# A different order of VectorE's work at the ends of groups, and of the first two units' scores, in a fused attention and SwiGLU kernel

## The chip, the core and the metric

The kernel runs on one core of one Trainium2 chip. The metric is the device time of one execution in microseconds (us). The kernel before takes 995.05 us, the median of three runs (994.68 to 995.08). The profile is of one execution with a span of 992.9 us from the first to the last instruction; times inside it count from the start of that span.

## The reference: hashed attention, then a SwiGLU block

The inputs are q, k and v of 4 batches, 8 heads, 768 positions and 64 dimensions, a projection of 64 x 6, two weights of 512 x 1536 and one of 1536 x 512. Cut to what matters:

```python
q_bucket = sum(((q @ proj) > 0) * 2**arange(6))      # k_bucket likewise
scores = where(q_bucket[:, None] == k_bucket[None, :], q @ k.T / 8, -1e9)
attn = softmax(scores)                               # with 1e-9 added to the sum
x = (attn @ v) with heads side by side               # (3072, 512)
g = x @ w_gate
out = (g * sigmoid(g) * (x @ w_val)) @ w_out         # (3072, 512)
```

## The kernel before

Heads are handled in pairs, 16 pairs in all, four to a batch. A pair has two halves of 384 queries, a half has six units of 128 keys. For a unit, `score` puts q k^T of two heads into two PSUM banks, adds a product of hash bits that pushes down the pairs whose buckets differ, and lets ScalarE take the exponential. All these banks come from one pool of seven that are handed out in turn:

```python
banks = tile_pool(name="ps", bufs=7, space=PSUM)

def score(u):
    sc = [bank("sc")[:, 0:HQ] for _ in range(2)]
    for x, start in ((T, True), (bits, False)):
        if u < 2 and not start:
            prepare_pair(1)          # units 0 and 1: the transposes of the second halves of k, of q
        for h in range(2):
            nc.tensor.matmul(sc[h], x["k", n][rows, ks], x["q", n][rows, qs], start=start, stop=not start)
    for h in range(2):
        nc.scalar.activation(weights(u)[:, h, 0:HQ], sc[h], AF.Exp, ...)
```

`prepare_pair` issues the next step of a pair's preparation: a transpose of three blocks on TensorE and its copy on ScalarE into `qT` or `kT`, or a hash product (`hps`) and the signs of it on ScalarE. For the first pair the hash of the second halves is issued after unit 2.

The SwiGLU block of a batch follows when its four pairs are done, beside the attention of the next batch. It is cut into atoms in a list, and after each attention step some atoms are taken from the list. Both its products use Strassen's scheme with seven products in place of eight. The up product (`up`) has six groups of two hidden tiles each, f and f + 1, and two halves of the tokens, so four spots (m, half) for the gate (g = 0) and four for the value (g = 1). For batches after the first a group is nested: two of its seven products are split by the scheme once more (`deeper`, width 192), which needs sums of weight blocks (`weigh`, into `inner` or `words`). Those of the first nested product are the group's `ahead` work:

```python
ahead = [lambda: weigh(0)] if nested else []        # four sums of 128 x 128 on VectorE

def step(at):
    if at == 0:
        while first: first.pop(0)()                 # operand sums of the batch
        finish(ahead)
    for do in todo[at]: do(at)                      # products, adds of PSUM into tiles, copies
    if at == len(todo) - 1:
        look_ahead()                                # the next atom's ahead work, if it has any
        settle(at + NB)                             # the group's last gating operations

def look_ahead():
    if atoms:
        finish(getattr(atoms[0][1], "ahead", []))
```

A gating is ScalarE's tanh, then two operations on VectorE: `c<-th,c` (line 571) and `hid<-c,hid` (line 575). The adds of PSUM into tiles, the weight sums and the operand sums are all `plus` (line 597 in the profile), and the matmuls of both products are `product` (line 593).

The down product (`po`) of a batch has three chunks of tokens with seven products each. Its operand sums are made by `combine` in two parts, part 0 by `early()` at the last up atom and part 1 in the first down step:

```python
def chunk(i):
    def step(n):
        a11, a12, s3, a22 = parts(i, slice(None))
        if n == 0 and i == 0:
            while next(preparing, None): pass
            for which in (1, 2, 3): combine(0, which, 1)
        ...
        a, w, to = ((a11, b11, "a"), (s1, t1, "b"), (s2, t2, "a"), (a12, b21, "c"),
                    (s3, t3, "a"), (s4, b22, "b"), (a22, t4, "a"))[n]
        product(now[to], [(a[:, f], w[:, f]) for f in range(NFP)], n in (0, 1, 3))
        ...                                         # copy or add to the output tile, send it
        for part in range(2):
            if n == 0: combine(i, 4, part)
            elif n in (3, 4) and i + 1 < CH:
                for which in ((1,), (2, 3))[n - 3]: combine(i + 1, which, part)
    for n in range(NB):
        atoms.append((2, lambda n=n: step(n), n == NB - 1))

def push_ffn(b):
    up_strassen(x, b, first)
    at = len(atoms) - 1
    early = down_strassen(out_of)
    size, last, end = atoms[at]
    atoms[at] = (size, lambda: (early(), last()), end)
```

When the attention is over, the rest of the list, above all the six up groups and the down product of the last batch, is run by the last lines:

```python
for _, atom, _ in atoms:
    atom()
```

[...]

Of the kernel before, what the change touches and what calls it, by code (L numbers as in the profile page):

```python
# [13 lines left out]
AF = mybir.ActivationFunctionType  # L14
# [4 lines left out]
def kernel(  # L19
# [11 lines left out]
    nc = tc.nc  # L31
    PSUM = bass.MemoryType.PSUM
    B, H, S, D = q.shape
# [3 lines left out]
    CH = NCH // 2  # L37
    HQ = CH * P
    BLOCK = 32
    NP = H // 2  # L40
# [10 lines left out]
    OFF = 2.0**35  # L51
    SCALE = 1.0 / D**0.5
# [16 lines left out]
    def bank(name):  # L69
        return banks.tile([P, 512], FP32, tag="ps", name=name)  # L70
# [98 lines left out]
    for h in range(2):  # L169
        rows = slice(h * D, (h + 1) * D)  # L170
# [24 lines left out]
    NB = 7  # L195
# [67 lines left out]
    def as_words(t):  # L263
        return t.bitcast(I32).rearrange("p (f w) -> p f w", w=2)

    spots = [hid[:, half, m].rearrange("p f q -> p (f q)") for half in range(2) for m in range(2)]
    early = [as_words(t[:, 0 : 2 * PIECE]) for t in spots]
# [115 lines left out]
    T = {}  # L383
    bits = {}
    atoms = []
# [85 lines left out]
    units = [(n, half, c) for n in range(len(pairs)) for half in range(2) for c in range(NCH)]  # L471
# [9 lines left out]
    def weights(u):  # L481
        return ((early_ring if u < MOVE else late_ring) + ring)[u % NCH]

    def score(u):
        n, half, c = units[u]
        qs = slice(half * HQ, (half + 1) * HQ)
        ks = slice(c * P, (c + 1) * P)
        sc = [bank("sc")[:, 0:HQ] for _ in range(2)]
        for x, start in ((T, True), (bits, False)):
            if u < 2 and not start:  # L490
                prepare_pair(1)
            for h in range(2):
                rows = slice(h * D, (h + 1) * D)
                nc.tensor.matmul(sc[h], x["k", n][rows, ks], x["q", n][rows, qs],  # L494
                                 start=start, stop=not start)
        for h in range(2):
            nc.scalar.activation(weights(u)[:, h, 0:HQ], sc[h], AF.Exp,  # L497
                                 scale=SCALE * (OFF / 2 if n <= NP else 1.0))

    def attend(u):  # L500
        n, half, c = units[u]
# [27 lines left out]
    def total(n):  # L529

        b, pr = pairs[n]

        ps = av_ps.tile([P, 512], FP32, tag="av", name="sum") if b == 0 else bank("sum")
        t = [acc.pop((n, half)) for half in range(2)]
        for h in range(2):
            for half in range(2):
                g = (2 * h + half) * BLOCK
                nc.tensor.matmul(ps[g : g + BLOCK, 0:HQ], ones, t[half][:, h, :],  # L540
                                 start=True, stop=True)
        if b == 0:
            space = wo.rearrange("p f m -> p (f m)")
            space = space[:, n % 2 * 3 * HQ : (n % 2 + 1) * 3 * HQ].rearrange("p (x q) -> p x q", q=HQ)
            r, t = space[:, 2, :], space[:, 0:2, :]
        else:
            r, t = t[1][:, 0, :], t[0]
        nc.vector.reciprocal(r, ps[:, 0:HQ])
        for half in range(2):
            for h in range(2):  # L550
                g = (2 * h + half) * BLOCK
                for at in (h * D, h * D + BLOCK):
                    nc.sync.dma_start(t[at : at + BLOCK, half, :], r[g : g + BLOCK, :])
        waiting.append(lambda: norm(n, t))
        if pr == NP - 1:
            push_ffn(b)
# [33 lines left out]
    def product(ps, pairs_, start):  # L590

        for i, (a, x) in enumerate(pairs_):
            nc.tensor.matmul(ps, a, x, start=start and i == 0, stop=i == len(pairs_) - 1,  # L593
                             skip_group_check=True)

    def plus(o, a, b, op=ALU.add):
        nc.vector.tensor_tensor(o, a, b, op=op)  # L597
# [162 lines left out]
        for i in range(NG // 2):  # L760
            both(i)

    def down_strassen(out_of):


        t2, t3, t4 = down_t
        t1 = b12
        s2, s1, s4 = down_s

        def parts(i, fs):  # L770
            return [hid[:, half, m, fs, i * P : (i + 1) * P]
                    for half in range(2) for m in range(2)]

        def combine(i, which, part):
            fs = slice(part * NFP // 2, (part + 1) * NFP // 2)
            a11, a12, a21, a22 = parts(i, fs)
            if which == 1:
                plus(s1[:, fs], a21, a22)
            elif which == 2:
                plus(s2[:, fs], s1[:, fs], a11, ALU.subtract)  # L780
            elif which == 3:
                plus(a21, a11, a21, ALU.subtract)
            else:
                plus(s4[:, fs], a12, s2[:, fs], ALU.subtract)

        def chunk(i):
            now = {}

            def step(n):
                a11, a12, s3, a22 = parts(i, slice(None))  # L790
                if n == 0 and i == 0:
                    while next(preparing, None):
                        pass
                    for which in (1, 2, 3):
                        combine(0, which, 1)
                if n == 0:
                    for name in "cba":
                        now[name] = bank("po")[:, 0:HD]
                    o = word_room[0]
                    now["o"] = [[o[:, (2 * r + x) * HD : (2 * r + x + 1) * HD] for x in range(2)]  # L800
                                for r in range(2)]
                a, w, to = ((a11, b11, "a"), (s1, t1, "b"), (s2, t2, "a"), (a12, b21, "c"),
                            (s3, t3, "a"), (s4, b22, "b"), (a22, t4, "a"))[n]
                c = now[to]
                product(c, [(a[:, f], w[:, f]) for f in range(NFP)], n in (0, 1, 3))
                r, x = ((0, 0), (1, 1), (0, 1), (0, 0), (1, 1), (0, 1), (1, 0))[n]
                o = now["o"][r][x]
                if n in (3, 4, 5):
                    plus(o, o, c)
                else:  # L810
                    nc.scalar.copy(o, c)  # L811
                if n >= 3:
                    nc.sync.dma_start(out_of(r, i)[:, x * HD : (x + 1) * HD], o)
                for part in range(2):
                    if n == 0:
                        combine(i, 4, part)
                    elif n in (3, 4) and i + 1 < CH:
                        for which in ((1,), (2, 3))[n - 3]:
                            combine(i + 1, which, part)

            for n in range(NB):
                atoms.append((2, lambda n=n: step(n), n == NB - 1))

        for i in range(CH):
            chunk(i)
        return lambda: [combine(0, which, 0) for which in (1, 2, 3)]

    def push_ffn(b):
        x = [xT[b, pr] for pr in range(NP)]
        rows = out[b * S : (b + 1) * S, :].rearrange("(p c) m -> p c m", c=NCH)  # L830

        def out_of(half, i):
            return rows[:, half * CH + i, :]

        up_strassen(x, b, first)
        at = len(atoms) - 1
        early = down_strassen(out_of)
        size, last, end = atoms[at]
        atoms[at] = (size, lambda: (early(), last()), end)

# [6 lines left out]
    def prepare_pair(count):  # L849
        for _ in range(count):  # L850
            rest.extend(f for f in steps.pop(0)() or [] if f)
# [5 lines left out]
    for u in range(0, N, NCH):  # L857
        n, half, _ = units[u]
# [5 lines left out]
        for c in range(NCH):  # L864
            score(u + c)
            if u + c == 2 or not gating and half == 1 and c == 2:
                prepare_pair(1)
            if c == 1 and half == 0 and 0 < n <= NP:
                total(n - 1)
            if c:  # L870
                add(u + c)
# [36 lines left out]
        end = True  # L908
        part = 0
        while atoms and (credit > 0 or not end):  # L910
            size, atom, end = atoms.pop(0)
# [11 lines left out]
            for _ in range(size):  # L923
                if chores:
                    step = chores.pop(0)
                    chores.extend(step and step() or [])
        while chores:
            step = chores.pop(0)
            chores.extend(step and step() or [])
    for _, atom, _ in atoms:  # L930
        atom()


# [30 lines left out]
```

The softmax here doesn't subtract the row's maximum and nothing guards it: scores larger than these inputs give would overflow.

## Time and profile before

The page of the profile and the lists behind it give this:

| what | value |
|---|---|
| time, median of 3 | 995.05 us |
| span of the profile | 992.9 us |
| ScalarE's waits for PSUM of the down product (line 811) | 180.1 us, 45 times |
| VectorE's waits for PSUM of the up product (line 597) | 76.5 and 41.6 us |
| TensorE's granted clock | 0.999 |
| up groups of batch 3 | from 822 to 933 us |
| down product of batch 3 | from 934 to 990 us |

Busy time says how long an engine had an instruction under way, and an average over the span hides single stages. A wait names the engine whose signal came last. Waits of an engine that isn't the bound cost nothing by themselves: ScalarE's 180.1 us above are such waits. The chain of work that ended last goes back from the last instruction to what released it, step by step; TensorE holds 91% of it, VectorE 5%, ScalarE 2%. In such a list a line has the start in us, the length in us, and the engine, the source line and what is written there; "x68" counts instructions that are merged in one line. An fp32 matmul stands as two records of equal length.

### The profile page before, as it was taken

The page shows a single profiled execution, that of the slowest core. Times are in us where ns is not written, and L with a number is a line of the kernel's source. Part 1 is how long each engine was busy: PE and PEld are TensorE (multiplying, and loading weights), DVE is VectorE, ACT ScalarE, POOL GpSimd, SP SyncE. Part 2 cuts the span into 40 slices and gives each one's busy share as a digit, 9 for nine tenths or more (in the row PEclk, how much of TensorE's full clock was granted, in tenths as well). Part 3 has the DMA queues.
Part 4 walks back from the last instruction along what each step waited for, and adds up shares of the span by engine and source line. Part 5 has one row for each costly group of instructions (what it writes and reads, how often), then busy time and mean ns, then how long its engine had stood idle before and what let it go on. Part 6 is the DMA issues. An engine that isn't in the chain of part 4 may idle for free.

```text
span 992.9 us, 13575 instructions
## 1 busy us (share of the span) xinstructions
PE 980.0 (99%) x4813; PEld 625.0 (63%) x4813; DVE 670.4 (68%) x1276; ACT 408.1 (41%) x921; POOL 127.3 (13%) x248
## 2 busy tenths in 40 slices
PE   9999999999999999999999999999999999999998
PEld 4444555555577766656566775666666786666687
DVE  5899888888965556777784457776776446667631
ACT  7999555566512234444442313443342202323200
POOL 3222232231100011111010001111100001121000
PEclk9999999999999999999999999999999999999999
DMA  8777685875303042433322114343121112233001
GB/s 235 218 249 229 157 259 178 228 269 157 106 26 76 16 121 79 104 92 84 99 81 57 52 31 108 98 107 100 57 87 33 35 34 85 75 117 105 1 30 35
DMA packets 119987, 107.02 MB, mean 108 GB/s; under 512 B 90032, under 2 KB 104848, under 8 KB 119920
## 3 DMA queue, kind: packets, MB, share of 16 engines
q0 software_dynamic: 18336, 73.29, 23.0%
q1 hardware_dynamic: 100784, 32.67, 14.2%
q8 instruction: 38, 0.62, 0.3%
q10 hardware_dynamic: 800, 0.20, 0.1%
q14 instruction: 29, 0.24, 0.1%
HBM read 81.79 MB, written 17.30 MB: 100 GB/s over the span
## 4 chain that ended last, share of the span: by engine, by line
PE 91%; DVE 5%; issue 2%; ACT 2%; POOL 0%; DMA 0%; DVEq 0%; ACTq 0%; POOLq 0%
PE up L593 41%; PE po L593 21%; PE sc L494 14%; PE av L509 11%; PE sum L540 1%; PE hps L412 1%; DVE c L571 1%; DVE hid L575 1%; PE tps L396 1%; DVE hid L597 1%; DVE room L368 0%; DVE inner L597 0%; PE idle L134 0%; DVE acc L527 0%; ACT th L570 0%
## 5 line engine op out<-in xcount | busy, mean ns | idle before, releaser
L593 PE MATMUL up<-xT,room 128*128 128x384 f32 (+1 forms) x732 | 243.0, 465 | 0.0
L593 PEld LDWEIGHTS up<-xT,room 128*128 128x128 f32 x732 | 134.8, 190 | 73.3 <-issue 9.8
L593 PE MATMUL up<-xc,room 128*128 128x384 f32 (+1 forms) x540 | 176.9, 455 | 0.0
L327 POOL DMA_DIRECT2D room<-ram x144 | 77.9, 543 | 677.8 <-PE up L593 662.4
L494 PE MATMUL sc<-qT,kT 64*128 64x384 f32 x768 | 161.0, 494 | 0.0
L597 DVE TENSOR_TENSOR c<-c,up 128x192 f32<-128x192 f32 (+1 forms) x198 | 78.9, 406 | 80.9 <-PE up L593 76.5
L527 DVE TENSOR_TENSOR acc<-acc,A 128x768 f32<-128x768 f32 x128 | 122.7, 958 | 15.7 <-ACT A L497 2.9
L593 PEld LDWEIGHTS up<-xc,room 128*128 128x128 f32 x540 | 99.2, 190 | 43.8 <-DVE c L597 1.1
L570 ACT ACTIVATE th<-c 128x384 f32<-128x384 f32 x90 | 46.9, 522 | 158.1 <-DVE c L571 89.7
L497 ACT ACTIVATE A<-sc 128x384 f32<-128x384 f32 x256 | 103.9, 528 | 0.6 <-PE sc L494 0.5
L494 PEld LDWEIGHTS sc<-qT,kT 64*128 64x128 f32 x768 | 67.9, 186 | 54.3 <-issue 40.5
L811 ACT COPY words<-po 128x256 f32<-128x256 f32 x48 | 17.9, 373 | 199.0 <-PE po L593 180.1
L597 DVE TENSOR_TENSOR hid<-hid,up 128x192 f32<-128x192 f32 (+1 forms) x162 | 67.5, 418 | 43.5 <-PE up L593 41.6
L509 PE MATMUL av<-A,vraw 128*64 128x384 f32 (+1 forms) x512 | 88.2, 486 | 0.0
L597 DVE TENSOR_TENSOR words<-words,po 128x256 f32<-128x256 f32 x36 | 15.2, 421 | 99.2 <-PE po L593 99.2
L679 ACT COPY c<-up 128x384 f32<-128x384 f32 x72 | 34.4, 478 | 88.8 <-PE up L593 88.7
L593 PE MATMUL po<-wo,room 128*128 128x256 f32 x288 | 66.6, 380 | 1.5 <-DVE room L597 1.5
L593 PE MATMUL po<-wo,hid 128*128 128x256 f32 x288 | 66.9, 382 | 0.0
L593 PE MATMUL po<-room,hid 128*128 128x256 f32 x288 | 66.1, 379 | 0.0
L509 PEld LDWEIGHTS av<-A,vraw 128*64 128x64 f32 x512 | 36.7, 137 | 46.1 <-issue 44.1
L494 PE MATMUL sc<-qb,kb 64*128 64x384 bf16 x384 | 65.1, 323 | 0.5 <-DVE kb L426 0.5
L593 PEld LDWEIGHTS po<-wo,hid 128*128 128x128 f32 x288 | 54.1, 190 | 12.1 <-issue 4.9
(137 smaller groups left out, 1165.3 us busy)
## 6 DMA issues: line engine op xcount, KB each, us to landing
room<-ram POOLq DMA_DIRECT2D x96, 384.0 KB, 3.7
vraw<-in_v_dram SPq DMA_DIRECT2D x16, 384.0 KB, 3.3
ram<-room POOLq DMA_DIRECT2D x12, 512.0 KB, 5.1
room<-ram POOLq DMA_DIRECT2D x48, 128.0 KB, 3.5
out_dram<-words SPq DMA_DIRECT2D x48, 128.0 KB, 1.7
room<-in_moe_w_out_dram POOLq DMA_DIRECT2D x10, 512.0 KB, 6.4
qraw<-in_q_dram SPq DMA_DIRECT2D x48, 96.0 KB, 3.2
hid<-in_moe_w_gate_dram POOLq DMA_DIRECT2D x9, 512.0 KB, 6.8
```

What stands on the lines that cost most here:

```text
L327: nc.gpsimd.dma_start(places[k % 2][:, PARTS[go], :], ram[k % NG][:, PARTS[go], :])
L396: nc.tensor.transpose(ps[:, i * P : (i + 1) * P], raws[name, n][:, half * CH + i, :, :].rearrange("p h d -> p (h d)"), ident)
L412: nc.tensor.matmul(tile_[i * BLOCK : (i + 1) * BLOCK, 0:HQ], hash_w, T[name, n][:, half * HQ : (half + 1) * HQ], start=True, stop=True)
L494: nc.tensor.matmul(sc[h], x["k", n][rows, ks], x["q", n][rows, qs], start=start, stop=not start)
L497: nc.scalar.activation(weights(u)[:, h, 0:HQ], sc[h], AF.Exp, scale=SCALE * (OFF / 2 if n <= NP else 1.0))
L509: nc.tensor.matmul(ps[h * D : (h + 1) * D, 0:width], raws["v", n][:, h, c, :], a[:, h, 0:width], start=c == 0, stop=c == NCH - 1)
L527: nc.vector.tensor_tensor(acc[n, half], acc[n, half], a[:, :, 0:HQ], op=ALU.add)
L570: nc.scalar.activation(th, g, AF.Tanh, scale=0.5)
L593: nc.tensor.matmul(ps, a, x, start=start and i == 0, stop=i == len(pairs_) - 1, skip_group_check=True)
L597: nc.vector.tensor_tensor(o, a, b, op=op)
L679: nc.scalar.copy(tile_of(g, spot), c)
L811: nc.scalar.copy(o, c)
```

## The change

It moves instructions and neither adds nor removes any. There are four parts.

- The tail takes each atom off the list before it runs it, so that `look_ahead` finds the next group there. Its purpose is that the weight sums of the next group are formed ahead of the last gating operations of the group before.
- In the last batch's down product the first chunk runs its products in the order 0, 3, 1, 2, 4, 5, 6. Its purpose is to give VectorE time for the operand sums that product 1 reads.
- `early()` is called after the last up atom of a batch in place of before it, except for the last batch. Its purpose is that the operations which free PSUM banks and feed the last tanh come first.
- For the first pair, the scores of unit 1 and the transposes of the second halves of both k and q are issued ahead of the bits of unit 0.

```diff
+    open_scores = {}
     def score(u):
+        n = units[u][0]
+        if u == 0:
+            for v in range(2):
+                score_part(v, T, True)
+                prepare_pair(1)
+        elif u > 1:
+            score_part(u, T, True)
+        score_part(u, bits, False)
+        for h in range(2):
+            nc.scalar.activation(weights(u)[:, h, 0:HQ], open_scores[u][h], AF.Exp, ...)
+
+    def score_part(u, x, start):
         n, half, c = units[u]
-        sc = [bank("sc")[:, 0:HQ] for _ in range(2)]
-        for x, start in ((T, True), (bits, False)):
-            if u < 2 and not start:
-                prepare_pair(1)
-            ...                      # matmuls and exponentials, now in the two functions
+        if start:
+            open_scores[u] = [bank("sc")[:, 0:HQ] for _ in range(2)]
+        sc = open_scores[u]
         ...
-    def down_strassen(out_of):
+    def down_strassen(out_of, at_once):
         ...
-            def step(n):
+            order = (0, 3, 1, 2, 4, 5, 6) if at_once and i == 0 else range(NB)
+            def step(at):
+                n = order[at]
         ...
-                    elif n in (3, 4) and i + 1 < CH:
-                        for which in ((1,), (2, 3))[n - 3]:
+                    elif at in (3, 4) and i + 1 < CH:
+                        for which in ((1,), (2, 3))[at - 3]:
         ...
-        early = down_strassen(out_of)
+        early = down_strassen(out_of, b == B - 1)
         size, last, end = atoms[at]
-        atoms[at] = (size, lambda: (early(), last()), end)
+        atoms[at] = (size, lambda: (early(), last()) if b == B - 1 else (last(), early()), end)
     ...
-    for _, atom, _ in atoms:
-        atom()
+    while atoms:
+        atoms.pop(0)[1]()
```

More of the change, by code (lines that the diff above doesn't have):

```diff
@@ L482, in weights @@
         return ((early_ring if u < MOVE else late_ring) + ring)[u % NCH]
+    open_scores = {}
     def score(u):
+        n = units[u][0]
[7 more added lines that the diff above has]
+        for h in range(2):
+            nc.scalar.activation(weights(u)[:, h, 0:HQ], open_scores[u][h], AF.Exp,
+                                 scale=SCALE * (OFF / 2 if n <= NP else 1.0))
+    def score_part(u, x, start):
         n, half, c = units[u]
@@ L487, in score @@
         ks = slice(c * P, (c + 1) * P)
-        sc = [bank("sc")[:, 0:HQ] for _ in range(2)]
-        for x, start in ((T, True), (bits, False)):
-            if u < 2 and not start:
-                prepare_pair(1)
[L492 to L495, printed above, removed]
+        if start:
+            open_scores[u] = [bank("sc")[:, 0:HQ] for _ in range(2)]
+        sc = open_scores[u]
         for h in range(2):
-            nc.scalar.activation(weights(u)[:, h, 0:HQ], sc[h], AF.Exp,
-                                 scale=SCALE * (OFF / 2 if n <= NP else 1.0))
+            rows = slice(h * D, (h + 1) * D)
+            nc.tensor.matmul(sc[h], x["k", n][rows, ks], x["q", n][rows, qs],
+                             start=start, stop=not start)
     def attend(u):
```

## The prediction

> **What bounds the kernel now.** I read the page's busy times first, then what TensorE waited for by its own wait list, then the chain of work that ended last, and last the timelines around each place where that chain leaves TensorE.
>
> The first line is the page's busy time; the next three are from the list of who waited for whom, cut to TensorE (waited for, total us, times, longest):
>
> ```profile
> PE 980.0 (99%) x4813; PEld 625.0 (63%) x4813; DVE 670.4 (68%) x1276; ACT 408.1 (41%) x921; POOL 127.3 (13%) x248
> ...
> PE up L593 <- DVE inner L597: 5.7, 5, 1.1
> PE po L593 <- DVE room L597: 1.5, 2, 1.0
> PE sc L494 <- DVE kb L426: 0.5, 1, 0.5
> ```
>
> TensorE is the bound over nearly all of the 992.9 us span, so no change that leaves its matmuls alone can win more than its holes. The list names them: five waits for VectorE's `inner` (the weight sums of the next group), two for `room` (the operand sums of the down product), one at the start for `kb` (the keys' bits).
>
> [...] a hole is larger than the wait shown. I therefore measure holes by starts. From the chain that ended last (start, us, what):
>
> ```profile
> 351.16 17.48 PE up L593 x68
> 368.64 5.05 PE sc L494 x36
> ...
> 507.17 3.47 PE sc L494 x21
> 510.64 0.04 issue
> 510.68 2.30 PE sc L494 x13
> 512.99 4.04 PE av L509 x24
> ...
> 881.43 14.86 PE up L593 x58
> 900.33 14.86 PE up L593 x58
> ```
>
> A nested group of 68 matmuls takes 17.48 us where nothing holds it. In the tail, groups follow each other every 900.33 - 881.43 = **18.90** us. So 1.42 us are lost per group end, 1.31 in the hole itself and 0.11 at the restart. Six scoring units take 5.05 us. Those after the last group of batch 1 take 512.99 - 507.17 = **5.82** us, so 0.77 are lost there, and a hole of the same shape stands at 751. The wait list calls neither a wait.
>
> VectorE's own order explains the tail. Timeline of the last group end (start, us, engine, line, operation, tiles):
>
> ```profile
> 915.22 0.56 DVE L597 TENSOR_TENSOR hid<-hid,up 128x384 f32<-128x384 f32 x1 [0.36 <-PE up L593]
> ...
> 916.15 0.55 DVE L575 SCALAR_TENSOR_TENSOR hid<-c,hid 128x384 f32<-128x384 f32 x1
> 916.27 0.52 ACT L570 ACTIVATE th<-c 128x384 f32<-128x384 f32 x1 [1.12 <-DVE c L571]
> ...
> 916.83 0.56 DVE L571 SCALAR_TENSOR_TENSOR c<-th,c 128x384 f32<-128x384 f32 x1
> 917.31 1.02 DVE L575 SCALAR_TENSOR_TENSOR hid<-c,hid 128x384 f32<-128x384 f32 x2
> ...
> 918.89 0.29 DVE L597 TENSOR_TENSOR inner<-inner,room 128x128 f32<-128x128 f32 x1
> ...
> 919.23 0.59 PE L593 MATMUL up<-xT,inner 128*128 128x192 f32 x2 [1.15 <-DVE inner L597]
> ```
>
> Three gating operations of the old group, one of them held by ScalarE's tanh, stand ahead of the four `inner` sums. TensorE has only two full products of the new group and one half-width product that need no sum; the last of their records starts at 917.76, so the next is due at 917.92.
>
> [...] here an exp lasts 0.53 and the next starts 0.37 to 0.39 after it. [...]
>
> **The change part by part.** No engine gets or loses an instruction. I compared the two built programs' orders: the shared ones of GpSimd and SyncE are equal; VectorE differs in eight places, TensorE and ScalarE in the first units, TensorE also in one down chunk.
>
> 1. *Emptying the list of atoms in the tail.* Before, the tail walked a list that never shrank, so look_ahead always saw its first atom. Now it sees the next group, and its four `inner` sums stand ahead of the three gating operations, at five group ends. They can start one issue after the gating operation of 916.15, at 916.15 + 0.46 = 916.61. The third sum, which TensorE needs first, started 0.65 after the first (918.24 to 918.89) and takes 0.30: done at 917.56, against a need at 917.92. The hole closes: 5 x 1.42 = **7.1 us**. What takes its place? The gating operations now end near 919.2, then VectorE adds the first inner product to its tile by about 919.5; TensorE overwrites that bank at 917.92 + 2 x 0.32 + 1.29 = 919.85. Margin 0.3 us, so I expect no new wait.
> 2. *Down product of the last batch, chunk 0: order 0, 3, 1, 2.* Product 1 waits half-way for the second half of s1. Twelve plus six records at 18.33/84 = 0.218 us are 3.93, but 938.95 - 933.91 = 5.04 passed: 1.1 lost and 0.1 at the restart. Product 3 (a12 by b21, 2.62 us) now fills it. It needs the last gated tile, ready at 938.3, for its last two records, at 933.91 + 22 x 0.218 = 938.7; s1 is ready at 938.9, needed at 940.4. Gain **1.2 us**, with a small margin on the gated tile.
> 3. *The early sums after the group's last operations, batches 0 to 2.* Three sums at some 0.5 us stood ahead of the adds that feed ScalarE's last tanh. That tanh started at 509.35, and the exps behind it at 509.78, 2.7 us after the first score; the fourth unit's second score needs the first exp's bank, at 507.1 + 2.5. Without the three the adds wait for the last up product alone: tanh near 508.25, exps near 508.7, bank free near 509.25 against 509.6. The hole closes in batches 1 and 2: 2 x 0.77 = **1.5 us**. In batch 0 the scores after the group already run in 5.05, and the hole at 280.4 is VectorE's backlog, which a swap of neighbours leaves: 0.
> 4. *The start.* ScalarE now copies the second half of qT before the first exp. From its timeline:
>
> ```profile
> 9.20 0.49 ACT L399 ACTIVATE kT<-tps 128x384 f32<-128x384 f32 x1 [0.69 <-PE tps L396]
> 9.59 0.87 ACT L497 ACTIVATE room<-sc 128x384 f32<-128x384 f32 x2
> 10.59 0.49 ACT L399 ACTIVATE qT<-tps 128x384 f32<-128x384 f32 x1
> 10.98 0.87 ACT L497 ACTIVATE room<-sc 128x384 f32<-128x384 f32 x2
> 11.72 0.89 ACT L497 ACTIVATE A<-sc 128x384 f32<-128x384 f32 x2
> 12.47 0.57 ACT L417 ACTIVATE kb<-hps,columns 32x384 bf16<-32x384 f32 x1
> ```
>
> Two exps fitted for nothing between the copies. Now all six follow qT, which starts some 0.17 earlier (one pair of bit matmuls left its front): exps from 10.42 + 0.39 = 10.8, six at 0.375 end the queue at 13.05, so the keys' sign comes 0.6 later than 12.47. The bank says the same: the third unit's second score takes the first exp's bank, free at 10.8 + 0.53 instead of before 10.66. TensorE waited at 12.97 to 13.79 for these bits; that point moves to about 14.4. A **loss of 0.6 us**, and TensorE is the bound from there on.
>
> Sum: -7.1 - 1.2 - 1.5 + 0.6 = **-9.2 us**; 995.05 - 9.2 = 985.85.
>
> **Rivals.** (a) *VectorE takes over in the tail.* It was busy 12.46 of 18.90 us there, 71% of 17.48; but its order now puts the adds that free inner banks behind the gating. If the 0.3 margin fails, each end keeps 0.2 to 0.5: 987 to 988. I hold this the likeliest miss. (b) *The next group's weights are not there early enough*, so the sums wait on a transfer. Issues land in 3.5 to 3.7 us, and the block the sums read is freed four steps, over 6 us, before the group's end; speaks against. If it held: 989 or more. (c) *The start gains.* Its purpose must be that the first unit's bits came late; in this trace those bit matmuls start at 9.10 right behind the transposes. If the loss vanished or turned, 984.8 to 985.3. A start loss could also be absorbed at two later waits of TensorE for ScalarE, near 33 and 55 us, worth 0.4 at most. (d) *The early sums delay the accumulators in batches 1 and 2*; they move by under half a microsecond and nothing on TensorE reads them within 20 us.
>
> **Range and chances.** Parts 1 to 3 are read off holes, which bounds the gain at 7.1 + 1.2 + 1.5 = 9.8; misses lie mostly above. So 985.8, range 984.8 to 987.5. The whole is 0.9%, far within 2%: a gain of 2% would need 19.9 us, more than all of TensorE's holes. Faster by over 2%: 0.01; within: 0.985; slower: 0.005.
>
> **What would show it.** Tail groups every 17.5 us and no wait for `inner`; no wait for `room` in the last chunk but the 0.5 at 280 still there; scores after batches 1 and 2 in 5.05; the wait for `kb` at the start longer, and a new wait for an exp's bank. Wrong if the tail groups stay near 17.9, or if the start is no later.

## The result and the profile after

The changed kernel takes 986.44 us (median of 986.24 to 986.53) against 995.07 us for the kernel before, run beside it: a ratio of 0.9914, 95% interval 0.9897 to 0.9931, or 8.6 us. The prediction said 985.8, range 984.8 to 987.5. The span of the profile falls from 992.9 to 984.6 us.

The list of who waited for whom in the changed kernel, cut to TensorE (waited for, total us, times, longest):

```profile
PE idle L134 <- DVE kb L131: 1.3, 1, 1.3
PE sc L509 <- DVE kb L426: 1.1, 1, 1.1
PE po L605 <- DVE room L609: 0.5, 1, 0.5
PE po L605 <- ACT words L827: 0.5, 1, 0.5
```

The five waits for `inner` and the wait for `room` in the last batch are gone; the 0.5 us for `room` after batch 0 is still there. Two things got worse: the wait for `kb` at the start has doubled, and a wait of the down product for ScalarE's `words` is new.

The chain that ended last, from the list of its longest pieces over the whole span (start, us, what):

```profile
508.01 5.05 PE sc L509 x36
517.09 18.33 PE po L605 x84
...
747.68 5.04 PE sc L509 x36
...
821.40 104.89 PE up L605 x408
926.29 10.37 PE po L605 x48
937.11 44.31 PE po L605 x204
```

The scores after batches 1 and 2 run in 5.05 us like all others. The six up groups of the tail, in six pieces before, are one piece of 408 matmuls; 104.89/6 = 17.48 us each. One piece means that the chain never leaves TensorE there. The down product breaks once, between 926.29 + 10.37 = 936.66 and 937.11.

To see where each microsecond went, I set the two traces' matmuls side by side, in their order, and note where the distance of their starts changes:

| place | change of the distance, us | predicted |
|---|---|---|
| start, up to the bits of unit 3 | +0.87, of which 0.21 before the first moved instruction | +0.6 |
| scores after batches 1 and 2 | -0.77 and -0.77 | -1.5 |
| five group ends of the tail, with their restarts | -7.09 | -7.1 |
| wait for s1 in the last down product, with its restart | -1.26 | -1.2 |
| new wait for ScalarE, with its restart | +0.73 | 0 |
| sum | -8.29 | -9.2 |

The last matmul starts 8.32 us earlier, as the two spans say. A restart is the longer distance between the first two matmuls after a wait (938.95 to 939.27 in the last down product before, so 0.32 us in place of 0.22). The loss at the start is not made up later: some 0.84 of the 0.87 us still stand at the scores after batch 1.

The 0.21 us come from TensorE's pace, not from the change. In both profiles the first transposes start at 5.14. The first line is of the kernel before, the second of the changed one:

```profile
5.14 0.61 PE L396 MATMUL tps<-ident,kraw 128*128 128x128 f32 x3
...
5.14 0.84 PE L396 MATMUL tps<-ident,kraw 128*128 128x128 f32 x3
```

After the change the six first transposes start 0.21 us apart; before, the distance falls to 0.12 and 0.11 after the second. In all twelve profiles TensorE's distances halve once in this way, at a moment between 4.0 and 7.1 us.

Timeline of the last up group end, the counterpart of the one shown of before:

```profile
909.78 0.55 DVE L587 SCALAR_TENSOR_TENSOR hid<-c,hid 128x384 f32<-128x384 f32 x1
...
910.25 0.29 DVE L609 TENSOR_TENSOR inner<-room 128x128 f32<-128x128 f32 x1
...
910.90 0.29 DVE L609 TENSOR_TENSOR inner<-inner,room 128x128 f32<-128x128 f32 x1
...
911.31 0.55 DVE L583 SCALAR_TENSOR_TENSOR c<-th,c 128x384 f32<-128x384 f32 x1
...
911.55 0.49 PE L605 MATMUL up<-xT,inner 128*128 128x192 f32 x2
```

The sums now start 0.47 us after the start of the gating operation, the third is done at 911.19, and TensorE takes it at 911.55 with no wait beside it: 0.36 us of slack. VectorE's starts have the order of the program: the four sums from 910.25 to 911.11, then gating from 911.31, where before gating started at 916.83 and 917.31 and the sums only from 918.24. A sum takes 0.28 to 0.29 us in both places.

The new wait, from the timeline of the last down product:

```profile
933.90 2.75 PE L605 MATMUL po<-room 128*128 128x256 f32 x12
...
936.69 0.37 ACT L827 COPY words<-po 128x256 f32<-128x256 f32 x1 [2.22 <-PE po L605]
937.11 2.46 PEld L605 LDWEIGHTS po<-room,hid 128*128 128x128 f32 x12 [0.86 <-ACT words L827]
937.11 2.86 PE L605 MATMUL po<-room,hid 128*128 128x256 f32 x12 [0.46 <-ACT words L827]
```

Product 2 fills bank a, ScalarE copies it out, and product 4 then adds into the same bank. In the plain order product 3 stands between them, in another bank. In the order 0, 3, 1, 2, 4 nothing does, and product 4 starts at 937.11, 0.05 us after the end of the copy that began at 936.69.

### The profile page after: what moved, and what is told of

The parts are those of the page before. It is cut to its first block, busy times and chain, and to the rows that moved or that the text cites. A ratio compares the mean times of both kernels' runs of the same rounds, so it can differ in the third digit from the quotient of the medians.

```text
span 984.6 us, 13575 instructions
## 1 busy us (share of the span) xinstructions
PE 977.8 (99%) x4813; PEld 624.2 (63%) x4813; DVE 669.4 (68%) x1276; ACT 408.4 (41%) x921; POOL 127.0 (13%) x248
## 4 chain that ended last, share of the span: by engine, by line
PE 94%; DVE 2%; issue 2%; ACT 1%; POOL 0%; DMA 0%; DVEq 0%; ACTq 0%; POOLq 0%
PE up L605 42%; PE po L605 22%; PE sc L509 14%; PE av L521 11%; PE sum L552 1%; PE hps L412 1%; PE tps L396 1%; DVE room L368 0%; PE idle L134 0%; DVE acc L539 0%; DMA room<-ram 0%; ACT A L497 0%; ACT kb L417 0%; ACT room L497 0%; DVE hid L587 0%
## 5 line engine op out<-in xcount | busy, mean ns | idle before, releaser
L509 PE MATMUL sc<-qb,kb 64*128 64x384 bf16 x384 | 63.0, 323 | 1.1 <-DVE kb L426 1.1
```

## The experiments

All times are medians beside fresh runs of the kernel before, which stood at 995.13, 995.05 and 994.94 us in the three sets. Differences are to the changed kernel's 986.44, which was timed in a set of its own. Repeats of one kernel lie up to 1.1 us apart, so differences of half a microsecond rest on the distances of starts in the traces as much as on the medians.

### The start back in its old order

```diff
-        if u == 0:
-            for v in range(2):
-                score_part(v, T, True)
-                prepare_pair(1)
+        for x, start in ((T, True), (bits, False)):
+            if u < 2 and not start:
+                prepare_pair(1)
```

> The changed kernel with the first two units' scores and exps back in the old order. Theory (ScalarE's queue): with the first pair of exps again between the copies of kT and qT, the keys' sign follows some 0.65 us earlier, so the bits of unit 3 start 0.65 us earlier and all of TensorE with them: 986.44 - 0.65 = 985.8 us. Rival (the later start comes from inputs that landed later in that one profile, the first transposes were 0.2 us late before any moved instruction): 986.2 to 986.4. Rival (the new order helps): 986.8 or more.

Measured: 985.89 us, 0.55 less. The new start is a loss, as predicted. In this profile the bits of unit 3 start at 13.79 against 14.66; 0.21 of that was there before any moved instruction, so 0.66 is the change's. The 0.21 are TensorE's pace again, and not late inputs as the rival had it: here the distances halve near 4.0 us, in the changed kernel's profile near 6.6. Old and new starts alike have early and late ones: the second hash product starts at 7.03, 7.04 and 7.23 in three profiles with the old start, at 7.03 to 7.40 in seven with the new. So I don't count this step to the change.

### Another order for the last chunk

```diff
-            order = (0, 3, 1, 2, 4, 5, 6) if at_once and i == 0 else range(NB)
+            order = (0, 3, 2, 1, 4, 5, 6) if at_once and i == 0 else range(NB)
```

> The changed kernel with the first chunk of the last down product in the order 0, 3, 2, 1, 4, 5, 6. Theory (product 4 adds into the bank that product 2 just filled and that ScalarE must first copy): product 1 now stands between them as product 3 did before, so TensorE's wait of 0.46 us for ScalarE near 937 us goes with its restart: 986.44 - 0.5 = 985.9 us. Rival (the wait only moves, to s2 for product 2, whose second half comes 0.6 us behind s1's): a wait for VectorE's room of 0.2 to 0.5 us, time unchanged.

Measured: 985.72 us, 0.72 less. The wait for ScalarE has gone from the list and no other has come. In the chain the whole down product is one piece:

```profile
821.44 104.90 PE up L605 x408
926.34 54.40 PE po L605 x252
```

Three chunks of 84 in 54.40 us. By starts the first chunk takes 18.13 us here, like the second, against 18.86 in the changed kernel: the wait and its restart were worth 0.73. The wait was the bank shared by products 2 and 4, and the rival (s2 late in turn) falls.

### The last chunk in plain order

```diff
-            order = (0, 3, 1, 2, 4, 5, 6) if at_once and i == 0 else range(NB)
+            order = range(NB)
```

> The changed kernel with the last down product back in the plain order. Theory: the wait for s1 returns (1.26 us by matmul starts) and the wait for ScalarE's copy goes (0.52): 986.44 + 0.74 = 987.2 us. Rival (the reordering is worth its full 1.2): 987.6.

Measured: 987.22 us, 0.78 more. Its list has the 1.0 us for `room` again and no wait for `words`. By starts the first chunk takes 19.39 us here against 18.86, so the reordering as it stands is worth 0.53 us: 1.26 taken away, 0.73 given back. The 0.78 of the medians agrees within the scatter of the repeats (986.88 to 987.54).

### The early sums in front again

```diff
-        atoms[at] = (size, lambda: (early(), last()) if b == B - 1 else (last(), early()), end)
+        atoms[at] = (size, lambda: (early(), last()), end)
```

> The changed kernel with the early sums ahead of the last up atom again in all batches. Theory (they hold the last tanh, behind it the exps, and with them the banks of the scores): 0.8 us are lost again after batches 1 and 2 and nothing after batch 0: 986.44 + 1.6 = 988.0 us. Rival (the gain there came from elsewhere, a shift of other work): 986.4 to 987.

Measured: 988.19 us, 1.75 more. The chain breaks again where it did, here after batch 1:

```profile
507.82 3.47 PE sc L509 x21
511.30 0.04 issue
511.33 2.31 PE sc L509 x13
513.64 4.04 PE av L521 x24
```

From 507.82 to 513.64 are 5.82 us as before the change, and after batch 2 it is the same: 0.77 us twice by starts. The changed kernel's own timeline shows the path: the tanh now starts at 509.10 and the exps behind it at 509.53, 1.6 us after the first score, where before it was 2.7.

```profile
507.94 0.92 PE L509 MATMUL sc<-qT,kT 64*128 64x384 f32 x4
508.05 0.56 DVE L609 TENSOR_TENSOR hid<-hid,up 128x384 f32<-128x384 f32 x1 [0.36 <-PE up L605]
...
509.10 0.52 ACT L582 ACTIVATE th<-c 128x384 f32<-128x384 f32 x1 [1.12 <-DVE c L583]
509.53 1.62 ACT L497 ACTIVATE room<-sc 128x384 f32<-128x384 f32 x4
```

The same place in the kernel before shows the bank that came late: the weights of the fourth unit's second score are loaded only after the first exp.

```profile
509.78 1.62 ACT L497 ACTIVATE room<-sc 128x384 f32<-128x384 f32 x4
...
510.30 0.18 PEld L494 LDWEIGHTS sc<-qT,kT 64*128 64x128 f32 x1 [0.48 <-ACT room L497]
```

### Emptying the list alone

The kernel before, with one edit:

```diff
-    for _, atom, _ in atoms:
-        atom()
+    while atoms:
+        atoms.pop(0)[1]()
```

> The kernel before with the list of atoms emptied in the tail, and nothing else. Theory (the five holes are the order of VectorE's sums and gating alone): 5 x 1.42 = 7.1 us less than before, 988.0 us; tail groups every 17.48 us. Rival (a part of the hole stays because VectorE's adds free the inner banks later): groups every 17.7 to 17.9 us, 989 to 990.

Measured: 988.15 us against 995.05 beside it, a ratio of 0.9932 (0.9920 to 0.9944): 6.9 us, four fifths of the whole change. The five holes close as in the full change, -1.4 us each by matmul starts. In this profile TensorE's distances halve near 6.5 us, close to the changed kernel's 6.6, and the second hash product starts at 7.23 against 7.03 before: 0.20 us later.

### Two more adds in front of the weight sums

```diff
     def look_ahead():
         if atoms:
+            if tail and getattr(atoms[0][1], "ahead", []):
+                for _ in range(2):
+                    plus(ring[0][:, 0, 0:HQ], ring[0][:, 1, 0:HQ], ring[0][:, 1, 0:HQ])
             finish(getattr(atoms[0][1], "ahead", []))
```

The tile is one of the attention weights, which nothing reads in the tail, so the output stays what it was.

> The changed kernel with two more VectorE adds of 128x384 ahead of the next group's weight sums at the five group ends of the tail (into a tile that nothing reads any more). Theory (TensorE needs the third sum 0.36 us after it is done, so there is that much slack and no more): each add takes one issue of 0.46 us, so 0.92 - 0.36 = 0.56 us of wait and 0.11 at the restart come back per end, 5 x 0.67 = 3.3 us: 989.8 us. Rival (VectorE has 30% idle in the tail, so two adds are hidden): 986.4 to 986.8. Rival (VectorE's order sets the whole group): 5 x 0.92 = 4.6 us or more.

Measured: 990.80 us, 4.36 more: between the theory's 3.3 and the last rival's 4.6. The trace says which:

```profile
PE up L610 <- DVE inner L614: 3.0, 5, 0.6
...
897.41 14.86 PE up L610 x58
915.75 14.85 PE up L610 x58
...
913.70 1.14 DVE L614 TENSOR_TENSOR A<-A 128x384 f32<-128x384 f32 x2
...
914.76 0.28 DVE L614 TENSOR_TENSOR inner<-room 128x128 f32<-128x128 f32 x1
...
915.41 0.29 DVE L614 TENSOR_TENSOR inner<-inner,room 128x128 f32<-128x128 f32 x1
...
915.75 0.59 PE L610 MATMUL up<-xT,inner 128*128 128x192 f32 x2 [0.59 <-DVE inner L614]
```

The two adds moved the sums by 914.76 - 913.70 = 1.06 us, not by 0.92: the second, which writes the tile of the first, started 1.14 - 0.55 = 0.6 after it, where 0.46 was expected. Groups now follow each other every 915.75 - 897.41 = 18.34 us, 0.86 more than 17.48: 0.76 of wait and 0.10 at the restart. So 1.06 - 0.76 = 0.30 us were hidden. That is the slack of 0.36 less the 0.05 us that pass from the end of the third sum (915.70) to the matmul that waited for it (915.75). In all 5 x 0.86 = 4.3. The theory of a small slack holds, my price of the adds was off. At that price the last rival would have asked for 5 x 1.06 = 5.3, so it falls too. VectorE's idle 30% of the tail hid nothing beyond the slack.

### The hash ahead of the exps

```diff
         score_part(u, bits, False)
+        if u == 1:
+            prepare_pair(1)              # hash of the second halves, their signs, the spread
...
-            if u + c == 2 or not gating and half == 1 and c == 2:
+            if not gating and half == 1 and c == 2:
```

> The changed kernel with the hash of the first pair's second halves, its signs and the spread of the keys' bits issued behind the bits of unit 1, ahead of the exps of units 1 and 2, in place of behind unit 2. Theory (the sign of the keys stands behind six exps in ScalarE's queue, and the bits of unit 3 wait for it): the sign then follows two exps, the wait of 1.1 us for kb falls to 0.2 or less: 986.44 - 0.9 = 985.5 us. Rival (TensorE itself is late there, through banks or inputs): the hash can't start earlier or the wait moves to the exps' banks: within 0.3 of 986.44.

Measured: 985.92 us, 0.52 less, between the theory's 0.9 and the rival's 0.3. Timelines of the start, first of the changed kernel:

```profile
10.74 0.49 ACT L399 ACTIVATE qT<-tps 128x384 f32<-128x384 f32 x1 [0.83 <-PE tps L396]
11.13 1.64 ACT L497 ACTIVATE room<-sc 128x384 f32<-128x384 f32 x4
12.61 0.92 ACT L497 ACTIVATE A<-sc 128x384 f32<-128x384 f32 x2
13.35 0.56 ACT L417 ACTIVATE kb<-hps,columns 32x384 bf16<-32x384 f32 x1
...
14.66 0.34 PE L509 MATMUL sc<-qb,kb 64*128 64x384 bf16 x2 [1.10 <-DVE kb L426]
```

then with the early hash:

```profile
11.29 0.87 ACT L499 ACTIVATE room<-sc 128x384 f32<-128x384 f32 x2
12.31 0.57 ACT L417 ACTIVATE kb<-hps,columns 32x384 bf16<-32x384 f32 x1 [0.16 <-PE hps L412]
12.91 0.57 ACT L417 ACTIVATE qb<-hps,columns 32x384 bf16<-32x384 f32 x1
13.51 0.87 ACT L499 ACTIVATE room<-sc 128x384 f32<-128x384 f32 x2
...
13.76 0.33 PE L511 MATMUL sc<-qb,kb 64*128 64x384 bf16 x2
```

In the changed kernel six exps (the 4 and the 2) stand between the copy of qT and the keys' sign, which starts at 13.35 though its hash product was out by 12.22 + 0.49 = 12.71. With the early hash it starts at 12.31 as soon as the product is there, and the wait for `kb` is gone: the bits of unit 3 start 0.9 us earlier, though TensorE's pace had made this profile 0.16 us late before the first moved instruction. That shows the queue of ScalarE as the cause. Of the 0.9 us some 0.2 are given back by the end of unit 5, after the exps of units 1 and 2, behind the signs now, have run later, and 0.1 near 243 us; I take the banks of those exps as the cause of the 0.2, but no wait in the list names it, so this is not shown.

### All together

The early hash, and the order 0, 3, 2, 1 in the first chunk of every batch:

```diff
-            order = (0, 3, 1, 2, 4, 5, 6) if at_once and i == 0 else range(NB)
+            order = (0, 3, 2, 1, 4, 5, 6) if i == 0 else range(NB)
```

> The early hash, and the order 0, 3, 2, 1, 4, 5, 6 in the first chunk of the down product of every batch. Theory: -0.9 at the start, -0.5 near 937 us, and the wait for room of 0.5 us and its restart after batch 0, where product 3 now covers the late sums: -0.6. 986.44 - 2.0 = 984.4 us. Rival (the sums after batch 0 are late for product 2 as well): 985.0.

Measured: 984.08 us (983.93 to 984.51), 2.4 less where 2.0 were expected, a ratio of 0.9891 (0.9877 to 0.9904) to the kernel before. All its runs lie below all runs of the changed kernel, though they weren't timed in the same set and the two ratios' intervals overlap. TensorE's list has two lines left:

```profile
PE idle L134 <- DVE kb L131: 1.3, 1, 1.3
PE sum L554 <- ACT xT L530: 0.2, 1, 0.2
```

The last `room` wait, after batch 0, is gone as well: matmul starts gained 0.75 us there, as against the expected 0.6, and 0.73 in the last chunk, as against 0.5. So after batch 0, too, the products had waited for late sums, and the change had mended this in the last batch only.

### The old start, without and with the early hash

Two more with the order 0, 3, 2, 1 in every batch's first chunk and the old start; the second has the hash behind the bits of unit 1.

> The old start of the first two units, and the order 0, 3, 2, 1, 4, 5, 6 in the first chunk of every batch. Theory (the terms add up): 986.44 - 0.55 (start, as measured alone) - 0.6 (last chunk) - 0.6 (chunk after batch 0) = 984.7 us. Rival (the start's loss is absorbed later or not at all, depending on the rest): 984.1 or 985.3.

> The same with the hash of the first pair's second halves behind the bits of unit 1, ahead of its exps, in the old order of the first two units. Theory (the sign of the keys is the only thing that TensorE waits for there): the wait of 0.5 us for kb goes and nothing takes its place: 984.7 - 0.5 = 984.2 us. Rival (the exps of unit 1 and 2, now behind two signs, free banks late, as with the early hash on the new start, where 0.3 of 0.9 came back so): 984.4 to 984.7.

Measured: 984.79 us (984.24 to 984.95) and 984.42 us (984.10 to 984.65). The terms add up in the first within 0.1 us, in part by luck: by starts the two chunks gave 0.73 and 0.76 in place of 0.6 each, and the profile has a new wait for a transfer of `qb` at 76.47 us, with a delay of 0.54. The second ends with no wait for `kb`, but its times overlap with those of the first, so whether it wins is open. The two profiles don't decide it: at the first product with v the second is 0.24 us later, 0.37 of delay having been there, by TensorE's pace, before the first moved instruction, and the first then loses the 0.54 at 76 us. With this order of products the three starts that ran lie within 0.7 us of each other. The start of the change was not run with it; with the change's own order, the old start and the early hash were 0.55 and 0.52 us faster than it.

## Why the prediction was right, and where it was not

The time was 0.6 us over the predicted 985.85. It came so near because TensorE's matmuls are the same in both kernels, so the change could only move holes, and each hole could be measured from starts. One term was left out of the sum (in 2), and one argument gave the right number for a wrong reason (in 4).

1. **The list of atoms.** Right in size (7.09 of 7.1), in mechanism and in margin: the third sum was done 0.36 us before its use, as worked out. The list emptied alone gave 6.9 us, and two adds in front of the sums took 4.4 back. The rival of inner banks freed too late, held the likeliest miss, did not come: the add that frees the bank ends at 913.06 and TensorE writes there at 913.49, a margin of 0.4 against 0.3, and groups run at 17.48, the bare matmuls.
2. **The last down product.** The hole closed as worked out (1.26), but the step "Product 3 now fills it" looked only at what product 1 waits for. It left out what product 3 had done in its old place: it covered ScalarE's copy of bank a between products 2 and 4. This term was missing from the sum, and it is 0.73 us, so the part gained 0.53 and not 1.2. With the order 0, 3, 2, 1 it vanished.
3. **The early sums.** Right: 1.54 against 1.5 by starts, and nothing after batch 0. Undoing it alone cost 1.75 by time and 1.54 by starts.
4. **The start.** A loss, right in sign and about in size: 0.55 by time when undone and 0.66 by starts, against 0.6. The queue argument was borne out, though qT's copy did not start 0.17 earlier as worked out: it started at 10.74, and without the 0.21 of TensorE's pace at 10.53, against 10.59 before. The second argument, that the third unit's second score would wait for the first exp's bank, was wrong. Its matmuls run without a break from 10.97, while the first exp only starts at 11.13:

```profile
10.97 0.81 PE L509 MATMUL sc<-qT,kT 64*128 64x384 f32 x4
11.62 0.33 PE L509 MATMUL sc<-qb,kb 64*128 64x384 bf16 x2
11.87 0.51 PE L412 MATMUL hps<-kT,hash 128*32 128x384 f32 x1
```

I had counted seven banks on in turn, so here the banks were not handed out strictly in turn; which bank that score took is not shown by the trace. Both arguments gave the same 0.6 us, so the number could not tell that one was false.

The forecast signs held: tail groups of 17.5, no wait for `inner`, the 0.5 at 280 still there, scores in 5.05, a longer wait for `kb`. The forecast "new wait for an exp's bank" did not come.

## What to carry to other kernels

Where one engine is busy 99% of the span, measure its holes by the distance of its starts and repair them by moving work on the engine that feeds it; four adds moved past three operations at five places were worth 7 us here. When an operation is moved to fill a hole, ask what it covered where it stood: here the moved product had hidden a copy of a bank, and more than half of its gain, 0.73 of 1.26 us, went there. A list that is walked instead of emptied can silently turn off a look-ahead; here the trace showed it as the same gap at every group end. Check each argument by the wait that it forecasts, and not only by its number.

## What was not expected of the hardware

Each of the holes in the up and down products costs more than the wait shown: at the tail's group ends before, 1.42 us by starts against 5.7/5 = 1.14 of wait, and in the last down product 1.26 against 1.0. In part this is the restart: the first pair of matmuls after it started 0.27 us apart instead of 0.16 in the up product, and 0.32 instead of 0.22 in the down product, so some 0.10 us per restart in both. TensorE's first matmuls ran at half pace (transposes 0.21 us apart, then 0.11 to 0.12), up to a moment that lay between 4.0 and 7.1 us in the twelve profiles; the start of the second hash product lay anywhere from 7.03 to 7.46 us, a spread as large as some of the effects measured here. And the two adds that write the same tile started 0.6 us apart, where the two `hid<-c,hid` of that size that follow each other at 911.78 in the changed kernel start 1.02 - 0.55 = 0.47 apart.
